# One matrix product per attention head, issued as one matmul or as four over column tiles

## Chip, core and metric

The kernel runs on one core of one Trainium2 chip. The metric is device time in microseconds (us), the median of several runs. The engines are TensorE (PE for matmuls, PEld for its weight loads), VectorE (DVE), ScalarE (ACT), GpSimd (POOL) and SyncE (SP, which issues most transfers).

## What is computed

Three layers follow one another. The first is a delta-rule attention over 4 batches, 8 heads, 768 steps and head size 48; the second a dense three-way max feed-forward layer; the third a mixture of 8 experts with the best two for each token. The part that the change touches is the attention:

```python
state = zeros((B, H, D, D))
for t in range(S):
    y[:, :, t] = einsum('bhd,bhde->bhe', q[:, :, t], state)
    v_old = einsum('bhde,bhd->bhe', state, k_n[:, :, t])
    state = state + bt * einsum('bhd,bhe->bhde', k_n[:, :, t], v[:, :, t] - v_old)
```

## The kernel before

The attention works in chunks of 64 tokens: 12 chunks in time and 4 batches make NS = 48 steps `s`. A step handles all 8 heads of two batches in turn (steps of even and odd number are two independent recurrences, each handing its state from `s` to `s + 2`). For a step, `gram` (lines 126 to 146) forms small products of keys and queries, with 32-column matmuls at L141; `norms` and `invert` (lines 92 to 183) invert triangular blocks on DVE for eight steps at once; `prep` (lines 232 to 256) forms the tile `tt` with four matmuls at L246 and calls `blend` (line 148), which fills the tile `M`: 112 rows, 8 heads, 112 columns.

`chain` (lines 263 to 290) is the recurrence itself. Its right operand is `z`, 112 rows (64 rows of values, 48 rows of state) by 8 heads by 48 columns. First come two halves (`blk`): in each, 8 matmuls of 112 rows by 32 columns at L274, which alternate between two column tiles 64 columns apart, and two copies by ACT back into `z` (L275 for even heads, L276 for odd ones). Then L279 makes the head's product: all 112 columns of `M` against `z`, one matmul for each head, into the PSUM tile `pf`. Rows 64 to 111 of `pf` are the new state, which DVE copies into the next `z` (L281); rows 0 to 63 are the output, which ACT copies to `y` (L286). POOL and DVE write the next `M` (L157) once L279 has read the old one; `M` and `tt` have two buffers each, the PSUM tile `pu` three.

All of this is in full float32, and in the trace every float32 matmul of the attention is two loads and two matmuls, so that the 8 products of a step are 16 records of L279, and 768 over the 48 steps. The feed-forward layer (`Moe1`, L408 and L429) uses another type, with one record for each matmul.

The order of the work: the loop at line 905 writes, for each step, `prep`, some feed-forward steps (a generator that `quota` meters by the number of finished steps), `chain`, more feed-forward steps, weight loading units and later `gram`s. The program order is a priority only: the framework plans the order of each engine's instructions with a timeline simulation of its own (`schedule_with_timeline_sim=True`, line 1009), so that feed-forward matmuls stand between the parts of a step on PE. The hardware then runs each engine's list in that order. After the 48 steps the last feed-forward group and the eight experts follow (`Moe2`, lines 573 to 703).

Of the kernel before, what the change touches and what calls it, by code (L numbers as in the profile page):

```python
# [54 lines left out]
class Attention:  # L55
# [207 lines left out]
    def chain(self, s):  # L263
        nc, st = self.nc, self.st[(s + OFF) // TB]
        cc = (s + OFF) % TB
        tt, m = st["tt"].pop(cc)
        z = self.zt(s)
        c = s % (2 * NCH) // 2
        pu = self.psum.tile([128, H, D], F32, name="pu", bufs=3)
        for blk in range(2):  # L270
            r = slice(32 * blk, 32 * blk + 32)
            for h in range(H):
                o = 32 * (blk + 2 * (h % 2))
                nc.tensor.matmul(pu[o:o + 32, h], tt[:, h, r], z[:, h], start=True, stop=True)  # L274
            nc.scalar.activation(z[r, 0:H:2], pu[r, 0:H:2], AF.Copy)  # L275
            nc.scalar.activation(z[r, 1:H:2], pu[32 * blk + 64:32 * blk + 96, 1:H:2], AF.Copy)  # L276
        pf = pu[0:112]
        for h in range(H):
            last = nc.tensor.matmul(pf[:, h], m[:, h], z[:, h], start=True, stop=True)  # L279
        if c < NCH - 1:  # L280
            nc.vector.tensor_copy(self.zt(s + 2)[64:112], pf[64:112])  # L281
        del self.Z[s]
        if c % 2 == 0:
            self.y[s % 2] = self.two.tile([128, DM], F32, name="y", bufs=YB)
        y = self.y[s % 2]
        nc.scalar.activation(y[64 * (c % 2):64 * (c % 2) + 64], pf[0:64].rearrange("p h e -> p (h e)"), AF.Copy,  # L286
                             scale=1.0 - 2.0 * (c % 2))
        if c % 2 == 1:
            self.on_rows(s // 24 * 12 + c // 2 * 2 + s % 2, y)
        return last  # L290
# [722 lines left out]
```

## Time and profile before

| | us |
|---|---|
| Median of 3 runs | 1167.8 |
| Lowest and highest run | 1165.3 and 1169.38 |
| Span of the profiled execution | 1163.1 |

The span runs from the first to the last instruction of one profiled execution; the execution's own time, with what lies around the span, is not listed apart, and the median of the runs is 4.7 us above the span. In the profile, L279 means line 279 of the kernel. A matmul's record lasts from its start to its modelled end, some 0.2 to 0.5 us, and several are in flight at once; the time that PE spends on a group is therefore read from start to start, and the busy time of a group counts overlapping records once. The attention stage below is the stretch from the first L279 to the last, 78.2 to 612 us.

### The profile page before, as it was taken

To read this page: it belongs to the slowest core of one execution; us is meant where nothing else is said; L and a number is where in the kernel's file an instruction comes from. 1 tells how busy PE (TensorE), PEld (TensorE's weight loads), DVE (VectorE), ACT (ScalarE), POOL (GpSimd) and SP (SyncE) were. 2 spreads that over 40 slices of the span, in tenths; PEclk is the share of its full clock that TensorE was granted. 3 is DMA by queue.
4 is the path that set the end of the run, shared out by engine and by line. 5 is a ranking of instruction groups with operands and counts; after the bars stand their busy time and mean duration, and the time that the engine had idled before them with its cause. 6 is when DMAs were issued, how large, how long until landed. Compare 5 with 4: busy or idle time off the path is not lost. (4 is left out here: it accounts for less than half of the span.)

```text
span 1163.1 us, 22982 instructions
## 1 busy us (share of the span) xinstructions
PE 1088.0 (94%) x9190; PEld 950.0 (82%) x9190; DVE 591.6 (51%) x1577; ACT 497.6 (43%) x1152; POOL 352.0 (30%) x308
## 2 busy tenths in 40 slices
PE   4579999989999999999999999999999999999995
PEld 3357888877887797888897979898989898989894
DVE  6864687959648836955226463424232424242210
ACT  4487427654563454455533233424242324242321
POOL 3333303232324314224212062424232323233221
PEclk9888899999999998999999999999999999999998
DMA  7768713464222122113105054534353534343121
GB/s 180 236 177 231 182 28 100 122 188 123 49 70 82 48 50 80 36 41 94 35 8 163 2 172 115 137 65 127 65 137 63 140 62 128 74 127 75 32 28 20
DMA packets 127076, 113.21 MB, mean 97 GB/s; under 512 B 76080, under 2 KB 115056, under 8 KB 126960
## 3 DMA queue, kind: packets, MB, share of 16 engines
q1 hardware_dynamic: 116080, 91.76, 28.8%
q0 software_dynamic: 10880, 19.89, 9.2%
q8 instruction: 74, 1.21, 0.5%
q14 instruction: 42, 0.34, 0.1%
HBM read 74.29 MB, written 37.33 MB: 96 GB/s over the span
## 5 line engine op out<-in xcount | busy, mean ns | idle before, releaser
L408 PE MATMUL pm<-xt,w 128*128 128x512 f32 (+1 forms) x1134 | 266.0, 383 | 3.0 <-ACT xt L385 1.7
L694 PE MATMUL py<-w,h 128*128 128x384 f32 (+1 forms) x1320 | 254.5, 342 | 2.5 <-ACT h L677 1.8
L694 PEld LDWEIGHTS py<-w,h 128*128 128x128 f32 (+1 forms) x1320 | 222.0, 181 | 15.6 <-ACT h L677 3.7
L672 PE MATMUL ph<-x,w 128*128 128x328 f32 (+1 forms) x1152 | 231.4, 352 | 1.9 <-DVE h L678 1.0
L408 PEld LDWEIGHTS pm<-xt,w 128*128 128x128 f32 x1134 | 196.2, 199 | 40.0 <-ACT xt L385 2.6
L672 PEld LDWEIGHTS ph<-x,w 128*128 128x128 f32 x1152 | 196.0, 188 | 22.9 <-DVE h L678 1.4
L678 DVE SCALAR_TENSOR_TENSOR h<-ph,h 128x328 fp32r<-128x328 f32 (+1 forms) x126 | 73.1, 590 | 175.9 <-ACT h L677 175.8
L698 POOL DMA_INDIRECT out_dram<-y,ix x56 | 87.1, 1555 | 231.9 <-ACT y L697 222.9
L621 POOL TENSOR_TENSOR w<-wst,w 128x768 fp32r<-128x768 f32 x32 | 62.9, 2105 | 132.4 <-ACT w L618 77.5
L677 ACT ACTIVATE h<-ph 128x328 fp32r<-128x328 f32 (+1 forms) x126 | 63.6, 514 | 75.2 <-PE ph L672 73.8
L697 ACT ACTIVATE y<-py,g 128x384 f32<-128x384 f32 (+1 forms) x56 | 31.7, 580 | 137.9 <-PE py L694 118.9
L429 PE MATMUL pm<-wo,h 128*128 128x400 f32 x432 | 89.1, 352 | 0.0
L279 PEld LDWEIGHTS pu<-z,M 112*112 112x112 f32 x768 | 82.6, 180 | 6.7 <-ACT z L276 2.1
L279 PE MATMUL pu<-z,M 112*112 112x48 f32 x768 | 83.4, 263 | 3.0 <-ACT z L276 1.7
L310 POOL TENSOR_TENSOR h<-mx,h 128x512 fp32r<-128x512 f32 (+1 forms) x36 | 40.6, 1128 | 127.0 <-ACT h L309 121.1
L429 PEld LDWEIGHTS pm<-wo,h 128*128 128x128 f32 x432 | 75.9, 188 | 2.2
L415 DVE TENSOR_TENSOR mx<-mx,pm 128x512 f32<-128x512 f32 (+1 forms) x84 | 51.0, 607 | 50.4 <-PE pm L408 48.9
L252 POOL TENSOR_TENSOR z<-z,nv 64x384 f32<-64x384 f32 x48 | 43.2, 905 | 102.0 <-DMA z<-in_v_dram 74.5
L180 DVE TENSOR_TENSOR T<-T,wide 128x31 f32<-128x31 f32 (+15 forms) x155 | 70.7, 456 | 4.4
L274 PEld LDWEIGHTS pu<-z,tt 112*32 112x32 f32 x1536 | 41.2, 112 | 33.7 <-issue 23.1
L565 POOL DMA_INDIRECT xd<-xr,si x48 | 50.5, 1052 | 60.0 <-issue 33.4
L274 PE MATMUL pu<-z,tt 112*32 112x48 f32 x1536 | 56.0, 213 | 11.9 <-issue 4.3
(168 smaller groups left out, 1294.7 us busy)
## 6 DMA issues: line engine op xcount, KB each, us to landing
wst<-in_moe_w_dram SPq DMA_DIRECT2D x24, 512.0 KB, 4.0
wst<-in_moe_w_dram SPq DMA_DIRECT2D x32, 384.0 KB, 3.7
xd<-zrow SPq DMA_DIRECT2D x8, 1361.5 KB
wld<-in_moe_w_dram SPq DMA_DIRECT2D x9, 768.0 KB, 8.3
xr<-xd SPq DMA_DIRECT2D x8, 778.0 KB, 4.5
x<-in_kq_dram SPq DMA_DIRECT2D x40, 144.0 KB, 2.6
out_dram<-zrow SPq DMA_DIRECT2D x6, 960.0 KB
xr<-xd SPq DMA_DIRECT2D x8, 583.5 KB, 5.6
```

The lines of the kernel that those rows point to most:

```text
L180: nc.vector.tensor_add(T[:, j + 1:, :m], T[:, j + 1:, :m], prv)
L274: nc.tensor.matmul(pu[o:o + 32, h], tt[:, h, r], z[:, h], start=True, stop=True)
L279: last = nc.tensor.matmul(pf[:, h], m[:, h], z[:, h], start=True, stop=True)
L408: mm = nc.tensor.matmul(pm, self.w[:, a, i, k, fs], x[:, b, k], start=(n == 0), stop=(n == 8))
L415: nc.vector.tensor_max(m, m, pm)
L429: nc.tensor.matmul(px, h[:, a, f, t * 128:(t + 1) * 128], self.wo[:, b, f], start=(n == 0), stop=(n == 3 * FT - 1))
L621: nc.gpsimd.tensor_sub(t[:, 1], x, t[:, 0].bitcast(F32))
L672: mm = nc.tensor.matmul(ph, w1[k][:, a, f * 128:(f + 1) * 128], x[:, b, k], start=(i == 0), stop=(i == 8))
L677: nc.scalar.activation(h[f][:, 0], ph, AF.Relu)
L678: nc.vector.scalar_tensor_tensor(h[f][:, 1], ph, 0.0, h[f][:, 0].bitcast(F32), op0=OP.max, op1=OP.subtract)
L694: nc.tensor.matmul(py[0:n], h[f][:, a, ts], w2[f // 2][:, b, f % 2], start=(i == 0), stop=(i == 23))
L698: st = nc.gpsimd.indirect_dma_start(out=self.ins["out"], out_offset=bass.IndirectOffsetOnAxis(ap=ix[0:n, t:t + 1], axis=0), in_=y[0:n], in ...
```

## The change

Each head's product at L279 is issued as four matmuls over the columns 0 to 31, 32 to 63, 64 to 95 and 96 to 111 of `M`, with the same right operand `z`; each writes the rows of `pf` with the same numbers. The result is the same sums in the same precision. Nothing else is touched.

```diff
         pf = pu[0:112]
         for h in range(H):
-            last = nc.tensor.matmul(pf[:, h], m[:, h], z[:, h], start=True, stop=True)
+            for o in range(0, 112, 32):
+                n = min(32, 112 - o)
+                last = nc.tensor.matmul(pf[o:o + n, h], m[:, h, o:o + n], z[:, h], start=True, stop=True)
```

## Rows read from the trace of the kernel before

**Rows 1.** Page, part 1: busy us, share of the span and instructions of each engine.
```profile
PE 1088.0 (94%) x9190; PEld 950.0 (82%) x9190; DVE 591.6 (51%) x1577; ACT 497.6 (43%) x1152; POOL 352.0 (30%) x308
```

**Rows 2.** Busy time of the engines before, in and after the attention stage (first line: columns).
```profile
core 0: us, PE busy (x) PEld busy (x) DVE busy (x) ACT busy (x) POOL busy (x), PEclk, DMA share, GB/s
0.00:78.20 78.20, 43.78 (x1003) 30.23 (x1003) 56.20 (x104) 42.57 (x89) 29.27 (x35) 0.89 0.70 194
78.20:612.00 533.80, 514.15 (x5277) 436.01 (x5277) 346.62 (x995) 276.92 (x738) 159.98 (x169) 0.96 0.34 89
612.00:1163.20 551.20, 530.04 (x2911) 483.73 (x2911) 188.74 (x480) 178.15 (x327) 162.78 (x105) 0.99 0.38 91
```

**Rows 3.** Groups of PE by line, 78.2 to 612 us: busy us, mean ns, idle before.
```profile
L408 PE MATMUL pm<-xt,w 128*128 128x512 f32 (+1 forms) x972 | 226.3, 380 | 2.4 <-ACT xt L385 1.1 <-DVE mx L415 0.8 <-DVE wg L358 0.3
L279 PE MATMUL pu<-z,M 112*112 112x48 f32 x768 | 83.4, 263 | 3.0 <-ACT z L276 1.7 <-issue 1.4
...
L274 PE MATMUL pu<-z,tt 112*32 112x48 f32 x1472 | 53.8, 212 | 8.5 <-issue 4.3 <-ACT z L276 2.2 <-DVE z L281 1.5
```

**Rows 4.** Timeline of PE, 544.5 to 547 us: start, length, line, operands, count.
```profile
545.01 0.50 PE L408 MATMUL pm<-xt,w 128*128 128x512 f32 x1
545.35 1.68 PE L279 MATMUL pu<-z,M 112*112 112x48 f32 x16
546.85 0.48 PE L408 MATMUL pm<-xt,w 128*128 128x512 f32 x1
```

**Rows 5.** Groups of weight loads (PEld) by line and shape, whole span.
```profile
L279 PEld LDWEIGHTS pu<-z,M 112*112 112x112 f32 x768 | 82.6, 180 | 6.7 <-ACT z L276 2.1 <-issue 1.9 <-POOL z L252 0.4
...
L274 PEld LDWEIGHTS pu<-z,tt 112*32 112x32 f32 x1536 | 41.2, 112 | 33.7 <-issue 23.1 <-ACT z L276 3.8 <-ACT P L142 0.7
```

**Rows 6.** Timeline of PE, 553 to 555.2 us.
```profile
553.57 0.60 PE L246 MATMUL pt<-R,G 128*112 128x128 f32 x4
554.10 0.53 PE L274 MATMUL pu<-z,tt 112*32 112x48 f32 x16
554.56 0.69 PE L246 MATMUL pt<-R,G 128*112 128x128 f32 x4
```

**Rows 7.** Matmuls of L274 alone in three short stretches; (x) counts those running.
```profile
554.16:554.18 0.02, 0.02 (x4) 1.00 0.00 0
554.20:554.22 0.02, 0.02 (x6) 1.00 0.00 0
554.24:554.26 0.02, 0.02 (x8) 1.00 0.00 0
```

**Rows 8.** Timeline of PE, 337.9 to 339.3 us.
```profile
338.18 0.86 PE L141 MATMUL pgr<-x 48*32 48x96 f32 x32
338.98 0.27 PE L274 MATMUL pu<-z,tt 112*32 112x48 f32 x2
```

**Rows 9.** Matmuls of L141 alone in three short stretches; (x) counts those running.
```profile
338.17:338.24 0.07, 0.06 (x4) 1.00 0.01 0
338.28:338.32 0.04, 0.04 (x8) 1.00 0.00 0
338.36:338.40 0.04, 0.04 (x12) 1.00 0.31 117
```

**Rows 10.** Timeline of PE, 41.6 to 42.4 us.
```profile
41.73 0.75 PE L213 MATMUL pu<-rc,P 32*32 32x32 f32 x64
```

**Rows 11.** Timeline of PE, 559 to 562 us.
```profile
559.68 1.68 PE L279 MATMUL pu<-z,M 112*112 112x48 f32 x16
561.29 0.53 PE L274 MATMUL pu<-z,tt 112*32 112x48 f32 x16
```

**Rows 12.** Timeline of PE, 339.5 to 342.9 us.
```profile
341.06 0.29 PE L274 MATMUL pu<-z,tt 112*32 112x48 f32 x3 [0.45 <-issue]
342.47 0.56 PE L274 MATMUL pu<-z,tt 112*32 112x48 f32 x16 [1.12 <-issue]
```

**Rows 13.** Page, part 3: DMA queue with packets, MB and share.
```profile
q8 instruction: 74, 1.21, 0.5%
```

## The prediction

> **What bounds the kernel now.** I read the busy shares first: PE is busy for 94% of the span, and no other engine for more than 51% [rows 1]. Such a share is a mean over stages, so the second view cuts the span at the first and last L279. In the attention stage, 78.2 to 612 us, PE is busy for 514 of 534 us; DVE has 347, ACT 277, POOL 160, and the DMA share is 0.34 [rows 2]. Before the stage PE has only 44 of 78 us, but no L279 runs there. So the change acts where PE sets the pace, and PE time taken out there should reach the end. The third view, the groups of PE in that stage, says what is at stake: the 768 matmuls of L279 hold 83.4 us, with only 3.0 us of idle time in front of them, which ACT's copies into z (L276) and issue end [rows 3].
>
> What bounds L279 itself is read from start to start. At 545.35 us its 16 matmuls begin, and the next line follows 1.50 us later [rows 4]: about 94 ns for each. The moving side is only 48 columns. L246 moves 128 columns through as large a stationary tile, and four of it take 0.53 us until the next line, which the first L274 then delays [rows 6]; so 48 columns cannot explain 94 ns, and the load of 112 stationary columns, back to back with the next one, does. A load lasts 180 ns in the trace with 112 columns and 112 ns with 32 [rows 5].
>
> **What the change removes and adds.** It removes 16 matmuls and 16 loads a step and adds 64 and 64, of 32 columns (16 in the last tile). No DMA is issued, no copy changes and no semaphore wait is added: L281, L286 and L157 wait for the last matmul of L279, as now.
>
> *Price of the new matmuls.* The nearest row is L274: the same 112 rows, 32 stationary and 48 moving columns, on two alternating column tiles. Its 16 matmuls take 0.46 us until the next line starts [rows 6]. The starts in the trace come in pairs, and the count of those running rises by two every 0.04 us, by the start times 42.5 ns [rows 7]: the two tiles run side by side, and a pair costs what one matmul does. Whether four do so too is shown by L141, whose q loop visits four column tiles: 32 matmuls of 96 columns take 0.80 us until the next line [rows 8], and the count of those running rises by four at a time, from 4 to 8 to 12 [rows 9], by the start times every 82.5 ns. That is the double for twice the columns, so with four tiles the moving side still sets the round, and loads of four tiles fit under it. L213, with 32 columns on four tiles, starts 64 in 0.75 us less the 0.19 of the last [rows 10], about 9 ns each, so issue allows four starts in some 36 ns. I take 42.5 ns for a round of four. The bounds: 36 ns from below (four starts at L213's rate) and 82.5 ns from above (L141's round, if the loads and not the columns set it). L274 is nearest in shape, hence its value.
>
> The Trainium skill (TensorEngine Tiling (Array Packing), Instruction Overhead) advises against this kind of change: a matmul has some 60 cycles of overhead, one that moves 1 column lasts as long as one that moves 60, and no tiling factor should be taken from a dimension that is already small. By it, as an estimate, 48 columns cost what 60 would, 42.5 x 60 / 48 = 53 ns for a round, 0.16 us more for a burst, and the sum for PE below would be 30 us and not 37. The trace does not agree: from 96 to 48 columns the round falls from 82.5 to 42.5 ns, with no floor at 60.
>
> A step has 8 heads in 2 passes, 16 rounds: 15 x 42.5 ns to the last round and 0.02 within it, 0.66 us.
>
> *Price of changing the tile width.* L246's four have starts 0.109 us apart, so the last of them starts at 553.90, and L274 follows 0.20 us behind it instead of 0.11; the last of L274 starts at 554.42 and L246 follows 0.14 us behind it instead of 0.04 [rows 6]. So going to narrow tiles costs 0.09 us, and coming back 0.09. A burst in wide company then takes 0.09 + 0.66 + 0.14 = 0.89 us against 1.50: 0.61 us saved, 29.5 us in 48 steps.
>
> *Neighbours.* Along the timeline of PE, 11 of the 48 bursts of L279 follow a burst of L141 or L274 and 21 precede one. There the kernel before pays the change of width (1.61 us from L279 to L274 instead of 1.50 [rows 4, 11]) and the new one pays none on that side. This is worth 0.11 us that goes and 0.09 to 0.14 that is not added, say 0.23 on 32 sides: 7.4 us. The sum for PE is 37 us. With 36 or 82.5 ns for a round it is 42 or 8 us (15 rounds x 40 ns more, 0.6 us on 48 steps, is 29 less).
>
> *What reaches the end.* PE stands still for 20 us of the stage, and some short waits are hidden inside its records. Where it waits for ACT, DVE or a transfer at a point of its ordered list, a faster burst only arrives earlier. The visible waits are 4% of the stage; I let 20% of the gain be lost, since DVE goes from 65 to 70% of the shorter stage and the planner will lay the list out anew. What is late next is the pair of copies L275 and L276 between the halves of L274. 0.8 x 37 = 30 us. The clock: granted 0.96 in the stage [rows 2]; I cost a change of it at nothing, between a gain of 5 us and a loss of 5 (0.01 of 534 us either way).
>
> The profiled execution has a span of 1163.1 us, 4.7 below the median of the runs; its own time beyond the span is not shown. 1163.1 - 30 = 1133, and with the same 4.7 us 1138 us.
>
> **Rivals.**
> (a) *The fourth tile stands apart.* It has 16 columns, and no row shows such a tile beside three of 32. If each pass then takes two rounds, a step has 32 rounds, 1.36 us, and the burst 1.36 + 0.09 + 0.09 = 1.54 us; less 0.15 for the neighbours (7.4 / 48) that is 0.11 below 1.50, 5 us in all and 4 at the end: 1164 us. For it: the odd size. Against: L141's rounds take whatever tiles come next.
> (b) *The stage stops being PE's.* PE's list is ordered, and the recurrence L274, ACT, L274, ACT, L279, L281 is a chain. If only a quarter to half of the 37 us come through, 9 to 18, the time is 1150 to 1159. Against: feed-forward matmuls are free to stand between, and PE idles for only 4%.
> (c) *Starts are serial*, the case in which the kernel gets slower. If each matmul needs a slot of its own, of the mean length of L274's, 0.46 / 16 = 29 ns, a burst takes 64 x 29 = 1.84, with the entry 1.93 us, less 0.15: 0.28 more than now, 13 us, 1181 us. It decides from (1.50 + 0.15 - 0.09) / 64 = 24 ns for each start. Against it stand L213's 9 ns and L141's four at a time [rows 9, 10].
> The Trainium skill (TensorE: Matmul & The Clock Gate, Wait — 56ns, not 53.3ns?) states a floor of about 25 ns from start to start. By it, as an estimate, the starts of a burst would take 64 x 25 = 1.60 us and the time would be about 1170; the trace does not agree, as L213's 9 ns shows.
> (d) *PE waits for its own instructions.* One queue carries 1.21 MB of instructions [rows 13], some 66 bytes for each of PE's 18,380, so it looks like PE's. The change adds 4,608, 25%, in bursts. There are stalls of PE within narrow bursts that nothing but issue ends, 0.45 to 1.12 us each [rows 12]. At 0.5 us on every burst 24 of the 37 us are lost, 0.8 x 13 = 10 stay, and the time is 1158; at 0.77 us nothing is left. For it: these stalls. Against: they are rare in the trace, 4.3 us before L274 in the whole stage [rows 3], and L213 issued its 64 without one [rows 10].
>
> **How the numbers follow.** About 0.3%, 3.5 us, is what a measurement of this kernel can tell from no change. The forecast, four tiles side by side, has 0.72 and a range of its own of 1124 to 1150; (a) 0.10, half of it within 0.3%; (b) 0.08; (c) 0.04; (d) 0.06, a third of it in each class. Faster: 0.72 + 0.05 + 0.08 + 0.02 = 0.87; same: 0.05 + 0.02 = 0.07; slower: 0.04 + 0.02 = 0.06. The predicted time is the forecast's, 1138. The range goes from 1122, which is the 42 us of the lower bound and some luck of the planner, to 1166, which takes in (a) and (b) and the price of 82.5 ns for a round (0.8 x 8 us, 1161).
>
> **What would show it.** Right: the group L279 with 3,072 matmuls, but 64 of them within about 0.9 us by the timeline; starts in fours, some 42 ns from four to four; the next wide line 0.14 us behind; a stage from the first to the last L279 of about 504 us in place of 534; the rest of the span unchanged at 551 us. Wrong: rounds of three and one (a); the same burst of 0.9 us with PE's idle time in the stage risen from 20 to 40 us or more (b); single starts 20 ns or more apart (c); more stalls that issue ends in front of L279 and L274 (d).

## The result, and the profile after

The changed kernel takes 1155.2 us (median of 6 runs, 1150.4 to 1161.5) against 1167.7 (6 runs, 1165.3 to 1169.4): a ratio of 0.990 with a 95% interval of 0.986 to 0.993. It is faster by 12.5 us, not by the 30 that were forecast; the direction was right, the size was not. The profiled execution of the changed kernel is its fastest run, 1150.4 us with a span of 1148.7, so the two profiled spans differ by 14.4 us and not by 12.5.

The changed line is L281 in the new kernel, and lines behind it move by two (L408 is now L410, L565 is L567). The page's first part:

```profile
PE 1062.4 (92%) x11494; PEld 914.2 (80%) x11494; DVE 597.2 (52%) x1577; ACT 497.6 (43%) x1152; POOL 355.3 (31%) x308
```

Busy time by stage, cut at the first and last L281 (columns as in [rows 2]):

```profile
78.90:600.80 521.90, 488.95 (x7581) 400.62 (x7581) 351.07 (x985) 277.11 (x739) 164.62 (x169) 0.94 0.35 92
600.80:1148.70 547.90, 528.51 (x2911) 482.63 (x2911) 189.83 (x490) 178.11 (x327) 162.69 (x105) 0.99 0.38 92
```

The stage is 522 us and not 504; PE is busy 25 us less, but it stands still for 33 us and not 20 [rows 2], and its clock is 0.94 of full and not 0.96. Behind the stage the span is 548 us, 3 less than before.

An ordinary burst on the timeline of PE, and a count of running matmuls of L281 in three short stretches of it:

```profile
302.67 0.86 PE L410 MATMUL pm<-xt,w 128*128 128x512 f32 x3
303.46 0.88 PE L281 MATMUL pu<-z,M 112*32 112x48 f32 x64
304.27 0.97 PE L410 MATMUL pm<-xt,w 128*128 128x512 f32 x3
```
```profile
303.54:303.57 0.03, 0.03 (x8) 1.00 0.00 0
303.58:303.61 0.03, 0.03 (x12) 1.00 0.00 0
303.62:303.65 0.03, 0.03 (x16) 1.00 0.00 0
```

The next line starts 0.81 us after the burst, where 1.50 stood [rows 4] and 0.66 + 0.14 = 0.80 was forecast. The count rises by four every 0.04 us, the 16-column tile among the four. So the price of the new matmuls was right to a hundredth. Now a burst that was not foreseen, on the timelines of PE and of POOL:

```profile
519.50 1.03 PE L246 MATMUL pt<-R,G 128*112 128x128 f32 x8
520.47 0.86 PE L281 MATMUL pu<-z,M 112*32 112x48 f32 x42
521.80 0.21 PE L281 MATMUL pu<-z,M 112*32 112x48 f32 x1 [0.48 <-issue]
522.51 0.29 PE L281 MATMUL pu<-z,M 112*32 112x48 f32 x4 [0.50 <-issue]
523.27 0.24 PE L281 MATMUL pu<-z,M 112*16 112x48 f32 x2 [0.47 <-issue]
523.99 0.40 PE L281 MATMUL pu<-z,M 112*32 112x48 f32 x5 [0.48 <-issue]
525.44 0.48 PE L281 MATMUL pu<-z,M 112*16 112x48 f32 x10 [1.04 <-issue]
525.85 0.48 PE L385 MATMUL pm<-ident,y 128*128 128x128 f32 x1
```
```profile
519.70 1.00 POOL L567 DMA_INDIRECT xd<-xr,si  x1 [1.58 <-DVE si L554]
521.00 0.97 POOL L567 DMA_INDIRECT xd<-xr,si  x1 [0.31 <-issue]
522.27 0.97 POOL L567 DMA_INDIRECT xd<-xr,si  x1 [0.30 <-issue]
523.54 0.96 POOL L567 DMA_INDIRECT xd<-xr,si  x1 [0.30 <-issue]
```

The same 64 matmuls take 5.4 us. They stop again and again for about half a microsecond, with no semaphore to wait for ("issue"), while POOL runs the four indirect scatters that put finished rows into the experts' buffer. The last stop, the longest, ends 0.9 us behind the end of the last scatter's record (524.50). In the list of who waited for whom in this stage (total us, times, longest), PE's first entry is now:

```profile
PE pu L281 <- issue: 9.4, 18, 1.4
PE pu L274 <- ACT z L276: 4.7, 3, 3.4
PE pu L274 <- DVE z L283: 3.4, 2, 2.0
PE pu L274 <- issue: 3.2, 6, 1.1
PE pgr L141 <- issue: 2.7, 7, 0.5
```

Of the 9.4 us, 2.5 lie before 108 us, where no scatter has run yet (the first begins at 180 us); they come back in e2. Of the eight runs of four scatters in the stage, six have such stops of PE in L281, L274, L141 or L385.

Going through the timelines of both engines, four bursts of L281 lie in such a run of scatters, and they last 1.6, 3.3, 3.7 and 5.2 us from first to last start; most others last 0.68, and those that don't have stops before 108 us, other lines in between, or the lower clock (1.2 us at 437.7 us, granted 0.50). In the kernel before, six bursts of L279 overlap scatters and none is more than 0.1 us longer than the rest, for example the one of [rows 4], beside these two:

```profile
544.40 0.99 POOL L565 DMA_INDIRECT xd<-xr,si  x1 [4.86 <-DVE si L552]
545.70 0.97 POOL L565 DMA_INDIRECT xd<-xr,si  x1 [0.30 <-issue]
```

A wide burst asks for 32 instructions (16 loads, 16 matmuls) in 1.5 us, 21 for each microsecond; a narrow one asks for 128 in 0.68 us, 188. The starved burst above got 128 in 5.4 us, 24 for each on the average, but not evenly. Its first 42 matmuls start at full pace. Between the start of the first stop (521.33) and the end of the last (525.44) only 12 start, with their loads some 6 instructions a microsecond; in the starved bursts at 349.4 and 449.9 us it is 10 or 11. That is below the 21 of a wide burst too, so the rate alone does not explain why no wide burst stops. The number may: the four starved bursts start 40 to 48 matmuls, 80 to 96 instructions with the loads, before their first stop, and a wide burst needs 32 in all. This is an estimate that no run tests by itself; e3 has rows that fit.

The stalls of L274 at 339 us [rows 12] have the same company in the kernel before: indirect scatters run on POOL there from 336.8 to 341.6 us, and here, too, the last stop ends 0.8 us behind them. One of the four:

```profile
340.67 0.96 POOL L565 DMA_INDIRECT xd<-xr,si  x1 [0.30 <-issue]
```

Do PE's instructions arrive late from memory? The queue q8 carried 74 packets before [rows 13] and carries 92 now, 16,384 bytes each; the 18 more are 64 bytes for each of the 4,608 instructions added, so the queue is PE's. Around the burst at 449.9 us, which takes 3.7 us with four stops, the view of the DMA queues from 449 to 454 us lists these two (packets, MB, share) and no q8:

```profile
q0 software_dynamic: 167, 0.57, 30.4%
q14 instruction: 1, 0.01, 0.7%
```

So at least those stops did not end with the arrival of a packet of PE's instructions.

Behind the starved burst the clock falls to its lower level, 1.2 GHz. PE busy and granted clock in two stretches:

```profile
519.00:523.70 4.70, 3.07 (x61) 1.00 0.61 152
523.70:530.50 6.80, 5.47 (x45) 0.50 0.36 105
```

**Theory 1:** while POOL runs an indirect scatter, PE gets its instructions slowly, and narrow bursts, which use them up fastest, starve. **Theory 2:** the stage is not paced by PE any more, rival (b). **Theory 3:** a quarter more instructions are too many for PE's supply by themselves, rival (d) in its plain form.

### The profile page after: what moved, and what is told of

Same layout as the page of the kernel before. It is cut to its first block, busy times and chain, and to the rows that moved or that the text cites. A ratio compares the mean times of both kernels' runs of the same rounds, so it can differ in the third digit from the quotient of the medians.

```text
span 1148.7 us, 27587 instructions
## 1 busy us (share of the span) xinstructions
PE 1062.4 (92%) x11494; PEld 914.2 (80%) x11494; DVE 597.2 (52%) x1577; ACT 497.6 (43%) x1152; POOL 355.3 (31%) x308
## 3 DMA queue, kind: packets, MB, share of 16 engines
q0 software_dynamic: 10880, 19.89, 9.3%
## 5 line engine op out<-in xcount | busy, mean ns | idle before, releaser
L410 PE MATMUL pm<-xt,w 128*128 128x512 f32 (+1 forms) x1134 | 261.6, 382 | 2.7 <-ACT xt L387 1.2
L410 PEld LDWEIGHTS pm<-xt,w 128*128 128x128 f32 x1134 | 195.5, 198 | 40.7 <-ACT xt L387 1.8
L274 PEld LDWEIGHTS pu<-z,tt 112*32 112x32 f32 x1536 | 42.8, 115 | 36.6 <-issue 23.6
L274 PE MATMUL pu<-z,tt 112*32 112x48 f32 x1536 | 56.9, 216 | 14.6 <-ACT z L276 4.7
L157 POOL TENSOR_TENSOR M<-P,nmask 64x256 f32<-64x256 f32 x48 | 41.4, 863 | 92.0 <-PE pu L281 87.4
L180 DVE TENSOR_TENSOR T<-T,wide 128x31 f32<-128x31 f32 (+15 forms) x155 | 64.4, 416 | 4.3
L178 DVE TENSOR_TENSOR wide<-A,T 128x31 f32<-128x31 f32 (+15 forms) x155 | 63.8, 412 | 4.5
L246 PE MATMUL pt<-R,G 128*112 128x128 f32 x384 | 61.2, 304 | 2.1 <-ACT R L243 1.9
```

Source lines behind the costliest of these rows:

```text
L178: nc.vector.tensor_mul(prv, A[:, j, j + 1:, None].to_broadcast([128, n, m]), T[:, j, None, :m].to_broadcast([128, n, m]))
L180: nc.vector.tensor_add(T[:, j + 1:, :m], T[:, j + 1:, :m], prv)
L246: last = nc.tensor.matmul(pt[:, u], G[:, u], R[:, u], start=True, stop=True)
L410: mm = nc.tensor.matmul(pm, self.w[:, a, i, k, fs], x[:, b, k], start=(n == 0), stop=(n == 8))
```

## Experiments

Each ratio is to the kernel before on the same chip; that kernel took 1164.4 us beside e1 to e4, 1164.8 beside e5 to e8 and 1168.8 beside e9 and e10. Four variants (e1, e2, e6, e7) leave the routed rows out of the experts' input, so they do not compute the reference's output.

**e1 and e2: no scatters.** In `Route.scatter`, in the kernel before and in the changed one:

```diff
     def scatter(self, t):
+        return
         nc = self.nc
```

> The kernel before, with POOL's scatters of the routed rows left out (the experts then work on the fill rows, so the output is not the reference's). Theory 1 (while POOL's scatters run, PE is fed its instructions slowly, and narrow bursts, which use them up fastest, starve): the issue-ended stalls of the kernel before (about 6 us in the stage, with the low clock behind them) go, so 1155 to 1163 us. Theory 2 (the stage of the changed kernel is simply not paced by PE any more): little change from 1167, since the scatters are POOL's work.

> The changed kernel with the same scatters left out (the experts work on the fill rows). Theory 1: the stalls inside the bursts of the changed line (about 16 us in the profile of the changed kernel) go, and this kernel is 28 to 37 us faster than the kernel before without scatters, as the sum of PE's time said: about 1122 to 1133 us. Theory 2: the gain over the kernel before without scatters stays at 10 to 14 us. Theory 3 (25% more instructions are too many for PE's fetch, scatters or not): stalls of 0.6 us that no semaphore ends stay in those bursts, 10 us or more in all, and the gain stays below 20 us.

Measured: e1 1150.0 us, ratio 0.989 (0.987 to 0.991); e2 1123.7 us, ratio 0.966 (0.964 to 0.967). Without scatters the change is worth 26.3 us and not 12.5. e1 is faster than the 1155 to 1163 expected: it gains 14 us, where the waits that issue ended were 6.7 us of the stage in the kernel before; where the rest comes from stays open. PE's waits in the stage of e2 that issue ended, with two others; and of e1 the two that correspond:

```profile
PE pu L274 <- ACT z L276: 6.0, 4, 2.6
PE pu L274 <- DVE z L283: 4.8, 4, 1.9
PE pu L281 <- issue: 4.3, 6, 1.3
...
PE pm L359 <- issue: 1.8, 1, 1.8
```
```profile
PE pu L274 <- ACT z L276: 2.6, 3, 1.5
PE pu L274 <- DVE z L281: 1.2, 1, 1.2
```

Theory 2 falls, since the gain more than doubled. Theory 3 does not vanish but is small: 6.6 us of issue waits stay in e2, 4.9 of them before 122 us and the rest at 200 and from 453 to 456 us, with no scatter anywhere in the stage; e1 has none. The gain is just under the 28 to 37 that theory 1 named. Summed along the timeline of PE from each burst's first start to the next line's (each piece by itself where other lines split a burst), the bursts went from 78.2 us (e1) to 43.0 (e2), 35 us less, of which 26 arrive. Most of the rest is seen above: L274 waits longer for z, from ACT's and DVE's copies, 10.8 us and not 3.8. That is the recurrence itself, which a shorter burst no longer covers. Issue waits outside the bursts are another 2.3 us.

**e3: two tiles for each head.**

```diff
-            for o in range(0, 112, 32):
-                n = min(32, 112 - o)
+            for o in range(0, 112, 64):
+                n = min(64, 112 - o)
```

> Each head as two matmuls, columns 0 to 63 and 64 to 111, in place of four: 64 instructions of PE in a burst of 16 rounds and not 128. A round is set by a load of 64 columns, 64/112 of 94 ns = 54 ns, so a burst is about 0.86 us and 0.18 for the changes of width, against 1.50: some 22 us of PE's time saved instead of 37. Theory 1: fewer instructions wanted during scatters, about half the stalls: 1148 to 1155 us, near the changed kernel or better. Theory 2: as the changed kernel, within 3 us. If loads of two wide tiles don't run side by side: 1165 or more.

Measured: 1154.5 us, ratio 0.992 (0.990 to 0.994), level with four tiles. An ordinary burst, and one during scatters, on the timeline of PE:

```profile
368.57 1.13 PE L281 MATMUL pu<-z,M 112*64 112x48 f32 x32
369.63 1.19 PE L410 MATMUL pm<-xt,w 128*128 128x512 f32 x4
```
```profile
252.14 0.49 PE L281 MATMUL pu<-z,M 112*64 112x48 f32 x9
252.85 0.30 PE L281 MATMUL pu<-z,M 112*64 112x48 f32 x4 [0.23 <-issue]
253.58 0.20 PE L281 MATMUL pu<-z,M 112*64 112x48 f32 x1 [0.42 <-issue]
254.29 0.69 PE L281 MATMUL pu<-z,M 112*48 112x48 f32 x18 [0.51 <-issue]
```

The ordinary burst costs 1.06 us to the next line, 0.25 more than with four tiles, and the stalls give that back: the worst burst takes 2.6 us from first to last start, and summed as in e2 the bursts take 55.4 us against 54.8. Four bursts overlap scatters, and only the one above, which begins beside the last scatter of a run, stops. The other three go at the ordinary pace, 70 instructions a microsecond, for example this one and the second scatter of its run:

```profile
355.01 1.13 PE L281 MATMUL pu<-z,M 112*64 112x48 f32 x32
354.91 0.97 POOL L567 DMA_INDIRECT xd<-xr,si  x1 [0.30 <-issue]
```

Level here says that two different losses balance; e10 parts them.

**e4 and e8: scatters one at a time.** The result is the same; only the place of the scatters moves. `scatter` puts them on a list, and each step issues one, ordered behind that step's last matmul of L281 (e4) or behind its last matmul of the first half of L274 (e8), so that four no longer run in a row:

```diff
     def scatter(self, t):
-        nc = self.nc
         for k in range(2):
+            self.held.append((self.xr, self.si, t, k))
+        if self.done:
+            self.flush()
+
+    def flush(self, n=99, after=None):
+        nc = self.nc
+        for _ in range(min(n, len(self.held))):
+            xr, si, t, k = self.held.pop(0)
...
+            if after is not None:
+                order(self.tc, st, after)
...
                 mm = at.chain(s)
+                rt.flush(1, mm)
```

> The changed kernel; the scatters are held back and put in one for each step, each ordered behind the last matmul of the changed line of a step, so that no burst of that line lies inside a run of four scatters. Output as before. Theory 1: stalls inside the bursts of the changed line fall from 16 us to below 4, some stay in L274 and L141 behind it: 1135 to 1148 us. Theory 2: no gain over the changed kernel, or a loss of a few us from the later scatters. Theory 3: no gain.

> As e4, but each scatter is ordered behind the last matmul of the first half of L274 of a step, where PE mostly goes on to feed-forward matmuls while ACT copies. Theory 1: as e4 within 6 us, 1126 to 1138 us, better if fewer narrow bursts follow within 1.3 us of the scatter's start. Theory 2 and 3: no better than the changed kernel, 1150 or more.

Measured: e4 1131.8 us, ratio 0.973 (0.969 to 0.977); e8 1123.7 us, ratio 0.963 (0.955 to 0.971). Both are 2 to 3 us faster than the ranges of theory 1. e8 beats both kernels, by 31 us on the changed one, and is as fast as the changed kernel with no scatters at all. Its burst beside a single scatter, PE and then POOL (the changed line is L283 there):

```profile
500.75 1.04 PE L283 MATMUL pu<-z,M 112*32 112x48 f32 x64
501.72 0.55 PE L387 MATMUL pm<-ident,y 128*128 128x128 f32 x3
```
```profile
499.99 0.99 POOL L580 DMA_INDIRECT xd<-xr,si  x1 [1.59 <-DVE si L560]
501.34 0.82 POOL L252 TENSOR_TENSOR z<-z,nv 64x384 f32<-64x384 f32 x1 [0.36 <-issue]
```

Five bursts still meet a scatter, and the longest of them is 2.0 us from first to last start. The stage's clock is back at 0.97.

**e5 and e9: the controls.** The kernel before, with the scatters spread as in e4 and as in e8: the diff above, with one matmul for each head.

> The kernel before (one matmul for each head) with the scatters spread as in e4, one for each step behind the last matmul of L279's line. It parts what the spreading gives by itself from what the narrow tiles give. Theory 1: spreading takes away the 6 us of stalls and the low clock behind them, as leaving the scatters out did, so 1150 to 1158 us, and e4 is 20 to 26 us faster than this. If the gain of e4 is only the spreading's: within 8 us of e4.

> The kernel before (one matmul for each head) with the scatters spread as in e8, one for each step behind the first half of L274. The control for e8: Theory 1: 1148 to 1158 us, as with the scatters left out (e1, 1150), and 25 to 32 us above e8; the narrow tiles are then worth what they were worth without scatters. If e8's gain is the spreading's alone: within 8 us of e8's 1124.

Measured: e5 1160.9 us, ratio 0.997 (0.994 to 1.000), a little above the 1150 to 1158 expected; e9 1153.6 us, ratio 0.988 (0.983 to 0.993). Spreading alone is worth 4 to 15 us to the wide kernel. By the medians e4 is 29 us below e5, where 20 to 26 was expected, and e8 30 below e9; each pair stood on two chips, and by the ratios it is 28 and 29. So the narrow tiles are worth nearly their 30 us, once no run of scatters lies over their bursts.

**e6 and e7: plain transfers in place of indirect ones,** with the same 128 rows and bytes, to rows that nothing reads, issued by POOL (e6) or ACT (e7):

```diff
-            st = nc.gpsimd.indirect_dma_start(
-                out=self.xd, out_offset=bass.IndirectOffsetOnAxis(ap=self.si[:, t, k:k + 1], axis=0),
-                in_=self.xr[:, t, 0:RW], in_offset=None)
...
+            n = len(self.scatters)
+            r0 = n % E * REG + 1024 + n // E * 128
+            self.scatters.append(nc.gpsimd.dma_start(self.xd[r0:r0 + 128], self.xr[:, t, 0:RW]))
```

> The changed kernel with every indirect scatter replaced by a plain transfer of the same 128 rows, issued by POOL at the same point, to rows of the buffer that nothing reads (the experts work on the fill rows). The same bytes move at the same times; what is gone is the indirect addressing. Theory 1a (the indirect instruction that POOL runs, about 1.05 us each, holds up PE's supply): stalls of the changed line gone, 1120 to 1130 us as in e2. Theory 1b (the transfers' traffic holds it up): stalls as in the changed kernel, 1145 to 1157 us.

> As e6, with the plain transfers issued by ACT and not by POOL. Theory 1a: 1120 to 1135 us (ACT may lose a few us to waiting for the rows). Theory 1b: 1145 to 1160 us. If e6 shows the stalls and this does not, it is POOL's issuing and neither the indirect addressing nor the bytes.

Measured: e6 1125.8 us, ratio 0.965 (0.957 to 0.972); e7 1125.9 us, 0.965 (0.958 to 0.972). Theory 1a holds as far as this goes: it is the indirect transfer, not the bytes (POOL's queue q0 moves 10,880 packets and 19.89 MB in e6 as in the changed kernel) and not POOL's issuing. Whether POOL's indirect instruction does it or the scattered rows it writes, e6 and e7 do not part, as both go. In e6 nine runs of four plain transfers begin in the stage, and no wait of PE that issue ended lies in one or within 1 us behind it; such waits are left elsewhere, 5.2 us before 124 us and 2.7 later, much as in e2. Four bursts overlap the plain transfers and none stops; one of them, PE and then POOL:

```profile
574.38 0.88 PE L281 MATMUL pu<-z,M 112*32 112x48 f32 x64
575.19 0.18 PE L544 MATMUL pgr<-os,tri 128*128 128x16 bf16 x1
```
```profile
573.20 2.19 POOL L569 DMA_DIRECT2D xd<-xr  x4 [13.76 <-issue]
```

Four plain transfers take 2.2 us and four indirect ones 4.8 (519.70 to 524.50 above), so part of the difference may be that fewer bursts are met; that the met ones run at full speed, and that L274 and L141 beside the other runs do not stop either, is what counts. What the indirect transfer takes from PE's supply no run shows.

**e10: two tiles, scatters spread as in e8.**

> Two column tiles of 64 and 48 for each head (as e3) with the scatters spread as in e8. Theory 1: without the stalls the order of the variants is that of PE's own time: bursts of 0.91 us and 0.68, so this is 8 to 12 us slower than e8, 1131 to 1136 us, though with the scatters in runs of four it was level with the changed kernel. If fewer instructions help by themselves, with no scatter near: as e8 or faster.

Measured: 1134.7 us, ratio 0.973 (0.969 to 0.977), 11 us above e8. With the scatters spread the two variants part by about what their ordinary bursts differ, 48 x 0.25 = 12 us; summed over all bursts, with the stops that are left, it is 52.0 against 44.2, 8 us.

## Why the prediction was wrong

*What bounds the stage, and L279.* Right: PE's pace, and the loads of 112 columns. Four loads of 32 columns run side by side. e3 bears the reading out: with 64 columns in a tile and the same 48 moving columns, the 16 rounds take 0.91 us from first to last start, some 60 ns each, and not 42.5.

*Price of the new matmuls.* Right: 0.68 us from first to last start against 0.66, rounds of four every 0.04 us, no slot for each start (rival c), no fourth tile apart (rival a). The Trainium skill (TensorEngine Tiling (Array Packing), Instruction Overhead) gives each matmul an overhead of some 60 cycles. By the prediction's estimate from it a burst would have taken 0.16 us more than 0.66; it took 0.02 more. That section's advice against tiling a dimension that is already small does not speak against this change, which splits the 112 columns and not the 48. The Trainium skill (TensorE: Matmul & The Clock Gate, Wait — 56ns, not 53.3ns?) states a floor of about 25 ns from start to start. The trace does not agree: 64 starts in 0.68 us are 11 ns each.

*Price of changing the width, and neighbours.* Right: 0.14 us to the next wide line, and from a wide L410 to the first L281 0.32 us where L408 to L279 took 0.23, so 0.09 for going to narrow tiles. The sum of 37 us for PE stands beside 35 where no scatter disturbs it (e1 to e2).

*What reaches the end.* Without scatters the factor of 0.8 was near: 26 of 35 us, 0.75. The reason that was named, ACT's copies between the halves, is about half of it (3.4 us more of waiting); DVE's copy of the state, which was not named, is as much (3.6 us).

*The step that failed* is the one that is missing from the sum: PE's supply of instructions was costed at nothing in the forecast. Of the 17.5 us between the 30 forecast and the 12.5 measured, 14 come back when the scatters are left out (26.3, e1 to e2). It was rival (d), with a chance of 0.06, and it was held to be rare because the whole stage of the kernel before had 4.3 us of it. Its condition was not read: the rows of [rows 12] were taken for how often this happens, and POOL's timeline at the same moment was not laid beside them. It would have shown an indirect scatter under the stalls, and the question would have been how many of the new bursts fall under one. Four did. Summed as above, the bursts of the changed kernel take 54.8 us, where e2 has 43.0: 12 us of the 37 are lost there, 11 of them in these four. That the time of rival (d), 1158, lies near the measured 1155 is luck: it stood for half a microsecond lost on every burst. Stalls also grow in L141, from 0.8 to 2.7 us, and the clock falls behind the starved bursts; from 0.96 to 0.94 of 522 us that is at most 10 us, an upper estimate, as not every instruction of PE follows the clock.

*The clock,* costed at nothing between a gain and a loss of 5 us, was not independent of this: it fell behind stalls, and without them it rose to 0.97.

## What to carry to other kernels

When one long matmul becomes many short ones, PE's demand for instructions is a cost of its own, by the number in a burst as well as by the rate: compare it, burst by burst, with stretches of the trace where issue alone ends PE's waits, and look at what the other engines do at those moments. Column tiles did halve a burst that the loads of its stationary side bounded, but more than half of that arrived only after POOL's indirect scatters had been taken out from under the bursts, one for each step behind a point where wide work follows. Two variants that measure the same may each lose something different; take the disturbance away and measure both again.

## What was not expected of the hardware

An indirect transfer on POOL (about 1 us each) slows the supply of instructions to PE, a different engine. During a run of four, narrow bursts went at full pace for 40 to 48 matmuls; then PE stopped for some 0.5 us at a time and got 6 to 11 instructions a microsecond. Plain transfers of the same rows from POOL did not slow it. No burst of 16 wide matmuls at L279 was held up, but single stops do stand in front of other wide lines (in the changed kernel 0.9 us in two at L385, in a run of scatters), so wide matmuls are not free of it.
